# An mLSTM with an ELU feed-forward layer on one core: TensorE durations of a planner, its order, and small products of ones in TensorE's early gaps

## The chip, the core and the metric

The kernel runs on one core of a Trainium2 chip. The metric is the device time of one execution in microseconds (us), as the median of several runs; lower is better. Engines have the profile's names: PE is TensorE's matmuls and PEld its weight loads, DVE is VectorE, ACT is ScalarE, POOL is GpSimd, SP is SyncE, whose queue issues the transfers.

## What is computed

The reference is an mLSTM recurrence over 768 steps for 4 batches and 8 heads of 40, and then a feed-forward layer over the 3072 rows (320 wide, 2048 hidden):

```python
for t in range(S):
    m_new = np.maximum(f_gate[:, :, t] + m, i_gate[:, :, t])
    f_stab = np.exp(f_gate[:, :, t] + m - m_new)
    i_stab = np.exp(i_gate[:, :, t] - m_new)
    m = m_new
    C = f_stab[:, :, None, None] * C + i_stab[:, :, None, None] * np.einsum('bhd,bhe->bhde', vt, kt)
    n = f_stab[:, :, None] * n + i_stab[:, :, None] * kt
    h_tilde = np.einsum('bhde,bhe->bhd', C, qt)
    denom = np.maximum(np.abs(np.einsum('bhd,bhd->bh', n, qt)[:, :, None]), 1.0)
    y[:, :, t] = 1.0 / (1.0 + np.exp(-o_gate[:, :, t])) * h_tilde / denom
...
h = x @ w_in
g = np.where(h > 0.0, h, np.exp(np.minimum(h, 0.0)) - 1.0)
return g @ w_out
```

## The kernel before

**Tiles of the first part.** The recurrence is computed in chunks of 128 steps. There are 6 chunks and 4 batches, so 24 tiles, t0 to t23, with t0 to t3 the first chunk. For a tile the kernel loads queries and keys (`qk`), values with keys and the output gate (`vko`), and, from the second chunk on, decays that are spread over the partitions (`bb`). TensorE forms 16 products of queries and keys (`products`, L597). For the first two chunks it also makes the decay matrix in logarithms, twice per tile (`spread`: L628 adds a mask, L632 and L638 the gates' sums); ScalarE takes its exponential (L653), and VectorE multiplies the products by it (L662). Then TensorE forms the outputs and what is added to the state (`outputs`, L682, L690, L700). VectorE and ScalarE make the denominators (L733 to L742), the result (L746), and TensorE turns it (`turn`, L763) for the second part. The gates of a chunk are prepared for all four batches at once on VectorE in `gate_chunk` (L454 to L492); they end in `lcs`, which `spread` reads.

**The weights.** `w_in` and `w_out` come in 18 pieces, c0 to c17, 512 or 640 columns each. Every piece is taken apart into an upper and a lower part for two-part products; that is some work for VectorE (L336, L341, L346, L361), for ScalarE (L327, L332, L357) and for GpSimd (L351). Pieces c0, c1, c5 and c6 have their lower part made by TensorE (L369, L370). c0, c1 and c2 hold the first quarter of `w_in` (c2 also the last 64 rows of the second quarter), c5 and c6 the second quarter, c9, c10 and c11 the third; c3 and c4 hold the first quarter of `w_out`, c7 and c8 the second.

**The second part.** The tiles are joined to blocks of 2 or 3. For a block and 128 of the hidden columns, one step is: 8 matmuls of the first layer (L816), relu and exponential on ScalarE (L824, L827), a combination on VectorE (L829), the upper part of the result on ScalarE (L832), the lower on VectorE or GpSimd (L834), and 3 matmuls per tile of the second layer (L843) into `acc`. The first block does hidden columns 0 to 7 (in units of 128) first, as do the second and the third.

**What sets the order.** No order is written out by hand. Every operation is entered as an `op` with a duration for each engine that may do it, and with what it reads and writes. `Plan.run` simulates the engines, the transfers and the buffers with these durations: at each moment it starts the ready operation with the lowest `rank`, and among equals that with the longest tail behind it. At the end it calls the operations in the order of their simulated starts. So each engine's order of instructions is fixed before the kernel runs, and each engine takes its instructions in that order. A transfer of `nbytes` takes `nbytes / 235e3` us of a common queue, which begins at 0.7, and lands 1.6 us later; a result is seen by another engine after `HOP`, 0.1 us.

**Ranks.** A string, `FIRST`, gives the first tiles and pieces their ranks 0, 1, 2 and so on. What is not in it gets a rank by the step of the second part that needs it (`lead`), and each step ranks behind what it needs.

Of the kernel before, what the change touches and what calls it, by code (L numbers as in the profile page):

```python
# [13 lines left out]
BF16 = mybir.dt.bfloat16  # L14
# [6 lines left out]
P = 128  # L21
# [16 lines left out]
class Plan:  # L38
# [11 lines left out]
    RATE = 235e3  # L50
    DEEP = 3.0
    BEGIN = 0.7

    def __init__(self, room, in_turn=()):
        self.room, self.in_turn = room, in_turn
# [4 lines left out]
    def op(self, engines, fn, r=(), w=(), nbytes=0):  # L60
        port = "port" in engines
        engines = {e: x for e, x in engines.items() if e != "port"}
        o = Op(engines, fn, {k[:2] for k in (*r, *w)}, nbytes, port)
        o.rank = self.rank
        for k in r:
            if k in self.writer:
                o.before.add(self.writer[k])
            self.readers.setdefault(k, []).append(o)
        for k in w:
            if k in self.writer:  # L70
                o.before.add(self.writer[k])
            o.before.update(self.readers.pop(k, ()))
            self.writer[k] = o
        o.before.discard(o)
        for b in o.before:
            b.after.add(o)
        self.ops.append(o)
        return o

    def run(self):  # L80
# [18 lines left out]
        queue, port, t, order, events = 0.0, 0.0, 0.0, [], {0.0}  # L99
# [16 lines left out]
        while len(order) < len(self.ops):  # L116
            assert events, "nothing can go on"
            t = min(events)
            events.discard(t)
            again = True  # L120
            while again:
# [12 lines left out]
                for o in ready:  # L134
# [40 lines left out]
                    again = True  # L175
                    break
        self.end = max(engines.values())
        self.order = order
        for _, _, e, o in order:
            o.fn(e)  # L180
# [3 lines left out]
def tile_mlstm_then_elu_ffn(  # L184
# [9 lines left out]
    nc = tc.nc  # L194
    PSUM = bass.MemoryType.PSUM
    B, NC, R3, _, HH, L = qk.shape
    D = 40
    DM, DFF = w_in.shape[1], w_in.shape[0] * w_in.shape[2]
# [18 lines left out]
    TMAX = max(BLOCKS)  # L217
    WMAX = max(512, W2N * DM)

    FIRST = "t0c0c4t1c1c5t2t4c3c7c11c9"  # L220

    LEAD, SPACE, LEAD_C = 4, 3, 0

# [3 lines left out]
    room = dict(  # L227
        wide=3, narrow=2, gates=2, qk=3, bb=3, vko=3, w=3, wl=2, dec=2, den=2, xf=2,
        x=3, ps_a=3, h=2, acc=3, e=2, gh=4, gl=4, os=3,
    )  # L230
    plan = Plan(room, ("qk", "bb", "e", "gh", "gl", "os"))
    op = plan.op
# [31 lines left out]
    def T(name, i, *shape, dt=F32, part=""):  # L264

        if (name, i, part) not in tiles:
            tiles[name, i, part] = pools[name].tile(list(shape), dt, name=name + part)
        return tiles[name, i, part]
# [111 lines left out]
    minus = const.tile([P, P], F32R, name="minus")  # L380

    m0 = const.tile([BH, 1], F32, name="m0")

    first = const.tile([BH, L], F32, name="first")

# [17 lines left out]

    def setup():
        nc.scalar.preload_act_table_set("natural_log_exp_and_others")
        op({"DVE": 0.1}, lambda e: nc.vector.memset(m0, -1e30), (), (("m0", 0),))
        op({"POOL": 1.6}, lambda e: make_identity(nc, ident), (), (("ident", 0),))
        op({"POOL": 0.2}, lambda e: nc.gpsimd.memset(first, 0.0), (), (("first", 0),))
        op({"ACT": 0.3}, lambda e: nc.scalar.mul(minus, ident, -1.0), (("ident", 0),), (("minus", 0),))

        def select(e):
            for j in range(3):
                rows = slice(j * BH, (j + 1) * BH)
                eng[e].tensor_copy(sel[rows], ident[rows, rows])

        op({"port": 1, "POOL": 0.8, "DVE": 0.4}, select, (("ident", 0),), (("sel", 0),))
        op({"ACT": 0.3, "POOL": 0.3, "DVE": 0.2}, lambda e: copy(e, ident_b, ident), (("ident", 0),), (("ident_b", 0),))

        def masked(e):
            nc.gpsimd.memset(mask, 0.0)  # L420
            nc.gpsimd.affine_select(
                out=mask, in_=mask, pattern=[[1, L]], compare_op=ALU.is_ge, fill=MASKED, base=0,
                channel_multiplier=-1,
            )

        op({"POOL": 0.6}, masked, (), (("mask", 0),))
        op({"POOL": 0.7, "DVE": 0.6},
           lambda e: eng[e].tensor_copy(ident4, ident.unsqueeze(1).to_broadcast([P, HH, L])),
           (("ident", 0),), (("ident4", 0),))

        plan.rank = rank[f"t{B}"] - 0.001
        for j, t in enumerate(bbs):
            op({"DVE": 0.52, "POOL": 0.56},
               lambda e, t=t: eng[e].memset(t[32:64], 0.0), (), (("bbzero", j),))
        plan.rank = rank["t0"]
        for b in range(B):
            op({"DVE": 0.3, "POOL": 0.4},
               lambda e, b=b: eng[e].memset(C[b], 0.0), (), (("C", b),))
# [116 lines left out]
    def attention(n):  # L555
        c, b = divmod(n, B)
# [42 lines left out]
                        start=True, stop=True,  # L599
                    )  # L600

        op({"PE": 1.25}, products, KQ + (("w", n, "room"),), tuple(("ps_a", (n, two)) for two in range(2)))

        if c < LOGS:
            op({"POOL": 0.2, "DVE": 0.08}, lambda e: eng[e].memset(va()[:, :, D:E], 1.0), (), (KV,))
# [69 lines left out]
        def outputs(e):  # L675
# [28 lines left out]
                            )  # L704

        KY = ("ps_a", (n, "y"))
        op({"PE": (1.6 if c else 0.9) + (0.36 if c < NC - 1 else 0.0)}, outputs,
           (("w", n, 0), ("w", n, 1), KV) + (KB + (("C", b),) if c else ())
           + ((KK,) if c < NC - 1 else ()), (KY, ("given", n)))
        if c < NC - 1:  # L710
# [54 lines left out]
                    start=(t == 0), stop=(t == 2), is_transpose=True, skip_group_check=True,  # L765
                )

        op({"PE": 0.55}, turn, (("xf", n), ("ident", 0)), (KTP,))
        op(act(3 * L), lambda e: nc.scalar.copy(xs("h"), ps("tp", P, 3, L)),
           (KTP,), (KX + ("h", slot),))  # L770
        if n < PARTS_BY_PE[0]:
# [139 lines left out]
    at = 0.0  # L911
# [23 lines left out]
        conversion(i)  # L935
    for u, (kb, f0, f1) in enumerate(units):
        ffn(u, kb, f0, f1)
    plan.run()


# [40 lines left out]
```

## Time and profile before

| what | value |
|---|---|
| median of 3 runs | 475.62 us (474.58 to 477.79) |
| the profiled execution's own time | 479.09 us |
| its span, first to last instruction | 477.1 us |
| mean granted TensorE clock in it | 0.981 |
| PE busy | 456.9 us, 5692 matmuls |
| DVE busy | 347.8 us |
| ACT busy | 303.1 us |
| POOL busy | 89.5 us |

Times in the profile are those of one execution, counted from the first instruction. A row of the timeline gives the start, the time, the engine, the line and the operands of an instruction or of a row of like ones, and in brackets how long the engine was idle before and which engine's instruction ended the wait. A row of the stretches gives the length of a stretch, the busy time and number of instructions of each engine in it, the granted clock as a share of full speed, the share of the transfer engines' time and GB/s. Matmuls are pipelined, so the time of one is longer than its distance to the next.

### The profile page before, as it was taken

Reading aid. Unit: us, or ns where it says so; the run is one execution under the profiler, and the core shown is the slowest. Engines: PE = TensorE matmul, PEld = TensorE weight load, DVE = VectorE, ACT = ScalarE, POOL = GpSimd, SP = SyncE. Lnnn points to the kernel's source line nnn. Section 1 sums busy time; section 2 is a strip of 40 time slices with the busy share of each in tenths; the row PEclk is TensorE's granted clock in tenths of the full one; section 3 lists DMA queues with packets and bytes.
Section 4 is the critical chain, followed back from the end, with each engine's and each line's share of the span. In section 5 each row is a group of like instructions: output and inputs, shape, how many; then the busy total and the mean of one; then the engine's idle time right before and its main releaser. Section 6 shows DMA issues by size and latency. Waiting matters only on the chain.

```text
span 477.1 us, 13768 instructions
## 1 busy us (share of the span) xinstructions
PE 456.9 (96%) x5692; PEld 428.4 (90%) x5692; DVE 347.8 (73%) x729; ACT 303.1 (64%) x743; POOL 89.5 (19%) x103
## 2 busy tenths in 40 slices
PE   5977999999999989999999999999999999999996
PEld 3645889899999989999989999999999999999996
DVE  7897899997869899638995768648875475456543
ACT  5886788897876556646465546655546564645764
POOL 2421244433213131003040122102110010000000
PEclk9796999999999999999999999999999999999999
DMA  8777465534143394113642334404432030100000
GB/s 261 259 225 233 134 214 170 153 116 153 41 137 97 105 278 138 43 40 98 185 144 71 101 94 134 133 3 139 140 101 82 1 101 1 43 1 3 28 1 27
DMA packets 39389, 52.83 MB, mean 111 GB/s; under 512 B 2880, under 2 KB 31264, under 8 KB 39328
## 3 DMA queue, kind: packets, MB, share of 16 engines
q1 hardware_dynamic: 39328, 51.97, 35.2%
q8 instruction: 44, 0.72, 0.6%
q14 instruction: 17, 0.14, 0.1%
HBM read 46.56 MB, written 5.39 MB: 109 GB/s over the span
## 4 chain that ended last, share of the span: by engine, by line
PE 80%; DVE 10%; DMA 3%; issue 2%; ACT 2%; POOL 1%; SPq 1%; DVEq 0%; ACTq 0%
PE h L816 34%; PE acc L843 32%; PE ps_a L597 4%; PE ps_a L690 3%; PE ps_a L682 2%; DMA wide<-in_w_in 2%; PE ps_a L763 1%; DMA w<-f_d 1%; PE h L628 1%; PE ps_a L700 1%; PE h L632 1%; PE h L638 1%; DVE w L645 1%; DMA bb<-b_d 1%; DVE gl L834 1%
## 5 line engine op out<-in xcount | busy, mean ns | idle before, releaser
L816 PE MATMUL h<-xh,w 128*128 128x384 f32 (+1 forms) x720 | 179.1, 323 | 0.4 <-ACT e L827 0.2
L843 PE MATMUL acc<-w,gh 128*128 128x320 f32 x768 | 173.4, 312 | 0.1
L843 PEld LDWEIGHTS acc<-w,gh 128*128 128x128 f32 x768 | 127.8, 188 | 2.4 <-ACT gh L832 0.3
L816 PEld LDWEIGHTS h<-xh,w 128*128 128x128 f32 x720 | 125.6, 189 | 2.7 <-DVE e L829 1.0
L829 DVE SCALAR_TENSOR_TENSOR e<-e,h 128x384 f32<-128x384 f32 (+1 forms) x144 | 72.5, 505 | 69.8 <-ACT e L827 69.2
L843 PE MATMUL acc<-w,gl 128*128 128x320 f32 x384 | 118.7, 309 | 0.4 <-DVE gl L834 0.4
L824 ACT ACTIVATE e<-h 128x384 f32<-128x384 f32 (+1 forms) x144 | 65.4, 454 | 78.0 <-PE h L816 74.9
L816 PE MATMUL h<-xl,w 128*128 128x384 f32 (+1 forms) x432 | 112.0, 318 | 0.0
L832 ACT CAST gh<-e 128x384 fp32r<-128x384 f32 (+1 forms) x144 | 67.7, 473 | 35.1 <-DVE e L829 34.0
L834 DVE TENSOR_TENSOR gl<-e,gh 128x384 fp32r<-128x384 f32 (+1 forms) x122 | 66.3, 547 | 32.1 <-ACT gh L832 30.2
L816 PEld LDWEIGHTS h<-xl,w 128*128 128x128 f32 x432 | 76.9, 189 | 0.0
L827 ACT ACTIVATE e<-e 128x384 f32<-128x384 f32 (+1 forms) x144 | 70.5, 490 | 4.0
L843 PEld LDWEIGHTS acc<-w,gl 128*128 128x128 f32 x384 | 72.0, 188 | 0.9 <-DVE gl L834 0.8
L834 POOL TENSOR_TENSOR gl<-e,gh 128x384 fp32r<-128x384 f32 (+1 forms) x22 | 24.4, 1115 | 109.0 <-ACT gh L832 95.6
L645 DVE TENSOR_TENSOR_SCAN w<-w,ident 128x512 f32<-128x512 f32 x32 | 39.1, 1225 | 4.6 <-DMA w<-f_d 4.6
L615 ACT ACTIVATE vko<-vko 128x320 f32<-128x320 f32 x72 | 33.5, 467 | 7.7 <-DMA vko<-in_vko 7.2
L597 PE MATMUL ps_a<-qk 40*128 40x128 f32 x384 | 31.0, 304 | 6.4 <-DMA qk<-in_qk 5.1
L351 POOL TENSOR_TENSOR narrow<-narrow,wide 128x512 int32<-128x512 int32 (+1 forms) x18 | 26.5, 1474 | 55.5 <-DVE narrow L346 25.9
L597 PEld LDWEIGHTS ps_a<-qk 40*128 40x128 f32 x384 | 25.9, 204 | 11.6 <-DMA qk<-in_qk 5.1
L662 DVE TENSOR_TENSOR w<-ps_a,w 128x512 f32<-128x512 f32 x48 | 31.6, 682 | 3.1 <-PE ps_a L597 2.7
L690 PE MATMUL ps_a<-vko,w 128*32 128x41 f32 x1536 | 20.3, 207 | 0.0
L690 PEld LDWEIGHTS ps_a<-vko,w 128*32 128x32 f32 x1536 | 18.6, 114 | 1.2 <-issue 1.1
(104 smaller groups left out, 413.9 us busy)
## 6 DMA issues: line engine op xcount, KB each, us to landing
vko<-in_vko SPq DMA_DIRECT2D x24, 484.0 KB
qk<-in_qk SPq DMA_DIRECT2D x24, 448.0 KB
w<-f_d SPq DMA_DIRECT2D x32, 256.0 KB
wide<-in_w_out SPq DMA_DIRECT2D x8, 640.0 KB
wide<-in_w_in SPq DMA_DIRECT2D x8, 512.0 KB
out<-os SPq DMA_DIRECT2D x24, 160.0 KB
bb<-b_d SPq DMA_DIRECT2D x40, 80.0 KB
sum<-os SPq DMA_DIRECT2D x8, 160.0 KB
```

The source lines that it names most:

```text
L597: nc.tensor.matmul(ps(two, P, HH, L)[:, j, :], kt[rows, j, :], qt[rows, j, :], start=True, stop=True,)
L615: lambda e, fn=fn, kw=kw: nc.scalar.activation(v3()[2], v3()[2], fn, **kw), (), (KS,))
L645: nc.vector.tensor_tensor_scan(a, a, ident4.rearrange("p h t -> p (h t)"), 0.0, op0=ALU.mult, op1=ALU.add)
L662: lambda e, half=half: nc.vector.tensor_mul(w(half), ps(half, P, HH, L), w(half)),
L690: nc.tensor.matmul(y[r, h, :], w()[:, i, r], va()[:, h, :], start=not opened, stop=(i == H - 1), skip_group_check=True,)
L816: nc.tensor.matmul(h(), a[g][:, fs], m, start=(i == 0), stop=(i == len(prods) - 1))
L824: op(act(N), lambda e, h=h, ff=ff: nc.scalar.activation(ff("e"), h(), AF.Relu, scale=-1.0), (KHP,), (KE,))
L827: lambda e, ff=ff: nc.scalar.activation(ff("e"), ff("e"), AF.Exp, scale=-1.0), (), (KE,))
L829: lambda e, h=h, ff=ff: nc.vector.scalar_tensor_tensor(out=ff("e"), in0=ff("e"), scalar=-1.0, in1=h(), op0=ALU.add, op1=ALU.max),
L832: op(act(N), lambda e, ff=ff: nc.scalar.copy(ff("gh", F32R), ff("e")), (KE,), (KG,))
L834: lambda e, ff=ff: eng[e].tensor_sub(ff("gl", F32R), ff("e"), ff("gh", F32R).bitcast(F32)),
L843: nc.tensor.matmul(acc(a), x[:, sl], bw[g][:, j, :], start=(f == f0 and i == 0), stop=(f == f1 - 1 and i == 2),)
```

## The change

Three things change. The planner's durations for `products`, `outputs` and `turn` on TensorE become shorter. `FIRST` becomes `t0 c0 c4 t1 c1 t2 t3 t4 c3 c7 c10 c11`: c5 and c9 leave it, t3 and c10 come in, and t3 stands ahead of t4. And a filler is added: a tile `ones` of 128 x 192 in bf16 is set to one, first on VectorE; when the plan is made, every gap on TensorE between the moment at which `ones` is there and the start of the first second-layer operation is given as many products of ones (128 rows, 128 weight columns, 192 columns) as fit in it less 0.1 us. They are counted at 0.165 us in the first gap and 0.09 us in the later ones. They write to columns of `acc` that nothing reads. They are not part of the simulation: it is over when they are put in, at the place in TensorE's order at which the gap begins.

```diff
+    FILL, FILL_COLD = 0.09, 0.165
+    filler = fill_from = fill_until = None
...
         self.end = max(engines.values())
+        if self.filler:
+            until = min(t for t, _, _, o in order if self.fill_until in o.touched)
+            begin = at = min(t + o.engines[e] for t, _, e, o in order if self.fill_from in o.touched) + self.HOP
+            more = []
+            for t, number, e, o in order:
+                if e == "PE" and t <= until:
+                    count = int((t - at - 0.1) / (self.FILL_COLD if at == begin else self.FILL))
+                    if count > 0:
+                        x = Op({"PE": t - at}, lambda e, count=count: self.filler(count), set(), 0, False)
+                        more.append((at, number, e, x))
+                    at = t + o.engines[e]
+            order = sorted(order + more, key=lambda x: x[0])
         self.order = order
...
-    FIRST = "t0c0c4t1c1c5t2t4c3c7c11c9"
+    FIRST = "t0c0c4t1c1t2t3t4c3c7c10c11"
...
+    ones = const.tile([P, 512 - DM], BF16, name="ones")
...
+        plan.rank = -1.0
+        op({"DVE": 0.1}, lambda e: nc.vector.memset(ones, 1.0), (), (("ones", 0),))
+        plan.rank = 0.0
...
-        op({"PE": 1.25}, products, KQ + (("w", n, "room"),), tuple(("ps_a", (n, two)) for two in range(2)))
+        op({"PE": 1.16}, products, KQ + (("w", n, "room"),), tuple(("ps_a", (n, two)) for two in range(2)))
...
-        op({"PE": (1.6 if c else 0.9) + (0.36 if c < NC - 1 else 0.0)}, outputs,
+        op({"PE": (1.38 if c else 0.8) + (0.32 if c < NC - 1 else 0.0)}, outputs,
...
-        op({"PE": 0.55}, turn, (("xf", n), ("ident", 0)), (KTP,))
+        op({"PE": 0.49}, turn, (("xf", n), ("ident", 0)), (KTP,))
...
+    def busy_work(count):
+        spare = T("acc", (0, 0), P, 512)[:, DM:]
+        for _ in range(count):
+            nc.tensor.matmul(spare, ones[:, 0:P], ones, start=True, stop=True, skip_group_check=True)
+
+    plan.filler, plan.fill_from, plan.fill_until = busy_work, ("ones", 0), ("turn", 2)
     plan.run()
```

## The prediction, made before the changed kernel ran

> **What bounds the kernel now.** I read the page first, then the busy time of each engine by stretches, then TensorE's timeline of the first 60 us, then VectorE's and what its idle time waited for. The page:
>
> ```profile
> span 477.1 us, 13768 instructions
> PE 456.9 (96%) x5692; PEld 428.4 (90%) x5692; DVE 347.8 (73%) x729; ACT 303.1 (64%) x743; POOL 89.5 (19%) x103
> PE   5977999999999989999999999999999999999996
> PEclk9796999999999999999999999999999999999999
> ```
>
> TensorE is busy 96% of the span and nearly all of its slack is in the first four slices of twelve us (and in the last, the drain). There the granted clock falls too. The stretches between its changes, and the rest of the run (columns: us in the stretch, PE, PEld, DVE, ACT, POOL busy, clock, DMA):
>
> ```profile
> 0.00:5.09 5.09, 0.00 (x0) 0.00 (x0) 3.75 (x15) 2.26 (x6) 2.26 (x11) 1.00 0.56 164
> 5.09:12.08 6.99, 6.70 (x36) 4.21 (x37) 4.85 (x17) 4.16 (x8) 0.40 (x1) 1.00 1.03 333
> 12.08:18.90 6.82, 5.67 (x139) 3.91 (x137) 5.33 (x13) 5.77 (x15) 2.40 (x3) 1.00 0.93 308
> 18.90:25.72 6.82, 6.82 (x122) 5.03 (x122) 5.64 (x15) 4.83 (x13) 2.93 (x3) 0.50 0.52 164
> 25.72:39.38 13.66, 8.04 (x136) 4.89 (x135) 12.99 (x34) 12.20 (x30) 3.39 (x3) 1.00 0.76 234
> 39.38:49.62 10.24, 8.89 (x135) 7.27 (x135) 7.27 (x18) 5.59 (x13) 2.53 (x3) 0.50 0.82 238
> 49.62:100.00 50.38, 49.62 (x825) 44.86 (x824) 46.48 (x97) 42.72 (x102) 18.88 (x19) 1.00 0.54 168
> 100.00:477.10 377.10, 371.19 (x4307) 358.19 (x4305) 261.47 (x527) 225.58 (x562) 56.73 (x61) 1.00 0.28 86
> ```
>
> From 49.62 on TensorE waits 0.76 us in 50 and 5.91 us in 377: whatever is gained ahead of 49.62 should stay gained, and little is to be had behind it. Two stretches show a clock of 0.50. A third is slow although its column says 1.00, which the durations show (TensorE's timeline: start, us, then the instruction):
>
> ```profile
> 5.09 2.08 PE L597 MATMUL ps_a<-qk 40*128 40x128 f32 x16 [5.09 <-DMA qk<-in_qk]
> ...
> 8.00 0.61 PE L632 MATMUL h<-sel,lcs 96*128 96x512 bf16 x1 [0.29 <-DVE lcs L490]
> 8.40 0.63 PE L638 MATMUL h<-lcs,sel 96*128 96x128 bf16 x4
> 8.83 0.63 PE L628 MATMUL h<-mask,ident_b 128*128 128x512 bf16 x1
> ...
> 12.61 0.38 PE L632 MATMUL h<-sel,lcs 96*128 96x512 bf16 x1
> 12.83 0.39 PE L638 MATMUL h<-lcs,sel 96*128 96x128 bf16 x4
> ...
> 14.94 1.16 PE L597 MATMUL ps_a<-qk 40*128 40x128 f32 x16
> ```
>
> The same 16 products take 2.08 us at 5.09 and 1.16 us at 14.94, so TensorE starts at half clock and keeps it until about 12. Cold busy time is 6.70 + 6.82 + 8.89 = 22.4 us; at full clock it would be 11.2. That is the most that a warm clock can give, and only if nothing else ended the waits. But in the front VectorE is nearly full: 12.99 of 13.66 us between 25.72 and 39.38. So what counts is VectorE's idle time that a cold TensorE caused (timeline of VectorE, idle before and its releaser in brackets):
>
> ```profile
> 9.70 0.17 DVE L236 COPY wl<-w 128x4 f32<-128x4 f32 x1 [1.62 <-ACT w L653]
> 14.31 0.67 DVE L236 COPY C<-ps_a 40x164 f32<-40x164 f32 x2 [1.01 <-PE ps_a L700]
> 22.72 1.29 DVE L662 TENSOR_TENSOR w<-ps_a,w 128x512 f32<-128x512 f32 x2 [0.54 <-PE ps_a L597]
> 24.48 0.67 DVE L236 COPY C<-ps_a 40x164 f32<-40x164 f32 x2 [0.40 <-PE ps_a L700]
> 42.84 0.17 DVE L236 COPY wl<-w 128x4 f32<-128x4 f32 x1 [0.41 <-ACT w L653]
> 44.12 0.17 DVE L236 COPY wl<-w 128x4 f32<-128x4 f32 x1 [0.77 <-ACT w L653]
> 45.49 1.29 DVE L662 TENSOR_TENSOR w<-ps_a,w 128x512 f32<-128x512 f32 x2 [1.21 <-PE ps_a L597]
> 50.17 0.42 DVE L829 SCALAR_TENSOR_TENSOR e<-e,h 128x256 f32<-128x256 f32 x1 [0.91 <-ACT e L827]
> ```
>
> Those released by ScalarE go back to TensorE as well: ScalarE's exponentials wait for the spread products, its relu for the first layer.
>
> **When the clock falls and rises.** Its visible changes lie on a grid of 3.41 us (18.90, 25.73, 39.38, 49.62), so I asked for the stretches of that grid:
>
> ```profile
> 15.49:18.90 3.41, 2.26 (x22) 1.34 (x18) 3.28 (x7) 3.36 (x8) 0.00 (x0) 1.00 0.97 329
> 18.90:22.32 3.42, 3.42 (x23) 2.49 (x23) 3.21 (x7) 3.39 (x10) 1.29 (x1) 0.50 0.52 160
> 29.14:32.55 3.41, 2.01 (x8) 0.96 (x10) 3.28 (x9) 3.22 (x9) 1.29 (x1) 1.00 1.02 280
> 35.97:39.38 3.41, 1.23 (x4) 0.47 (x3) 3.14 (x11) 2.56 (x7) 0.00 (x0) 1.00 0.58 202
> 42.79:46.21 3.42, 3.42 (x69) 2.97 (x71) 1.39 (x6) 2.49 (x5) 0.72 (x1) 0.50 0.83 238
> ```
>
> The clock fell behind stretches with 2.26 and 1.23 us of matmul, and not behind one with 2.01; it did not rise behind 18.90:22.32 or 42.79:46.21 although TensorE was full there, with two us of 40-row products in each. Busy time alone does not decide; what the array is given seems to count. The filler has 128 rows, so I expect it to count fully, which no row here shows.
>
> The longest gaps of TensorE ahead of the two falls:
>
> ```profile
> 17.05 0.67 PE L763 MATMUL ps_a<-ident,xf 128*128 128x128 f32 x3 [0.94 <-DVE xf L746]
> ...
> 40.73 0.59 PE L628 MATMUL h<-mask,ident_b 128*128 128x512 bf16 x1 [3.53 <-DVE e L829]
> ```
>
> The Trainium skill (TensorE: Matmul & The Clock Gate, section "Why this matters for your kernels") speaks against filling short gaps: only gaps above about 3 us are to bring the clock back to half. The trace differs, since the fall at 18.90 follows a gap of 0.94 us. By the rule that fall would have another cause than idling, the fill would not mend it, and the sum below would be the second stretch's 0.94 us smaller.
>
> **The change part by part.**
>
> *Fill at the head.* By its own constants the plan has the first products at about 4.49 us (0.7 to the queue's begin, 2.09 of gate and query bytes, 1.6 of landing, 0.1), the fill from 0.2, so (4.49 - 0.2 - 0.1) / 0.165 = 25 fillers. Their price: the four products of 128 columns at 8.40 take 0.43 us to the next start, 0.107 each cold, and one of 512 columns from 8.00 to 8.40 takes 0.40 to 0.43; by the line through both, 192 columns take about 0.16 us cold, and half of that warm. 25 of them are 4.0 us from about 1.1, so they end at 5.1 at the latest, where the products' data lands (5.09): free. If the clock has risen by 8.00, where the chain turns from VectorE's decay sums to TensorE, the first exponential comes 0.5 us earlier, and the first outputs 0.7 us earlier still (of the 1.01 at 14.31; ScalarE, 5.77 of 6.82 us busy behind 12.08, takes the rest of the 2 us that TensorE saves).
>
> *Second stretch.* Warm products and outputs give VectorE back 0.54 + 0.40 = 0.94 us.
>
> *Third stretch.* Of 0.41 I take 0.30, and 0.77 + 1.21 + 0.91 whole: 3.19 us. Halving TensorE's 8.89 us would allow 4.4; VectorE's own work takes the difference.
>
> Together 0.5 + 0.7 + 0.94 + 3.19 = 5.3 us, between nothing (clock as before) and 11.2 (TensorE alone decides).
>
> *What the fillers cost.* TensorE takes its instructions in order. A filler stands where the plan, not the chip, has a gap. In 5.09 to 49.62 TensorE is idle about 8.4 us now (the stretches' lengths less PE's time, rows above), and some 14 once its work there is 11.2 us shorter and the front 5.3; at 0.09 a filler, less what the rounding leaves, that is some 130 fillers.
>
> ```profile
> 29.99 0.96 DVE L737 TENSOR_SCALAR den<-den 128x8 f32<-128x8 f32 x1
> ```
>
> VectorE runs behind its plan there (this maximum and the reciprocal behind it are planned at 0.30 together), so most gaps will be as long as planned or longer, and the filler ends before the data. Where TensorE itself is late, a filler adds its length. Bounds: 0 and 5.2 us (half of 130 at 0.08 us, the excess when cold). I take 0.6, near the lower end, because VectorE is the fuller engine in the front. The memset of ones, first on VectorE, costs the 0.1 of its plan, and the chain starts on VectorE, so it counts whole. The head's rise may come too late for the first exponentials: 0 to 1.2, taken as 0.5.
>
> The Trainium skill (the same page, section "Part 1: The HAM clock gate") has one busy window of 3.4 us raise the clock. By that the head's fill has the clock up by 8.5 us at the latest; by the rows of 18.90:22.32, with 40-row products behind the fill, it may be a window later, and then the sum is 0.7 us less.
>
> *Order anew.* c5 (a quarter of w_in) leaves the ranks of the front, t3 comes ahead of t4, c10 stands in for c9 (same size). c5's steps now, with its transfer:
>
> ```profile
> 31.46 0.39 DVE L336 TENSOR_SCALAR narrow<-narrow 128x512 f32<-128x512 f32 x1
> 31.88 0.43 DVE L341 TENSOR_SCALAR narrow<-narrow 128x512 int32<-128x512 int32 x1
> 32.34 0.69 DVE L346 SCALAR_TENSOR_TENSOR narrow<-wide,narrow 128x512 int32<-128x512 int32 x1
> 20.45 0.33 SPq L322 DMA_DIRECT2D wide<-in_w_in  x1
> 50.27 0.46 PE L843 MATMUL acc<-w,gh 128*128 128x320 f32 x2
> ```
>
> 1.5 us of VectorE leave the stretch in which VectorE is full, and its transfer falls behind those of t2, t3, t4 and c3 on SP's queue. But it is needed for the fifth step of the first block, and between 49.62 and 100 VectorE has 46.48 of 50.38 us; t3's steps come forward in its place. Bounds +1.5 and -1.5; I take 0, as work is only exchanged.
>
> *Durations.* The plan's TensorE shrinks by 24 x 0.09 + 20 x 0.26 + 4 x 0.14 + 24 x 0.06, some 9 us; 1.16 for the products is what the row at 14.94 shows. No instruction changes, only the order of a greedy list. Behind 49.62 there are 6.7 us of idle TensorE in all, the drain behind the last matmul among them; so at best some 2 us, at worst a wait of the size of the front's, 1.2 us. I take 0.
>
> **The sum.** 5.3 - 0.1 - 0.6 - 0.5 = 4.1 us. The profiled execution took 479.09 us, of which 477.1 are its span: 475.0 after. The three runs shown have a median of 475.62, 3.5 us below the profiled one. If that offset belongs to profiling, the median becomes 471.5, which is my forecast. If it is the clock (the grid need not lie alike in every execution, and the runs spread over 3.2 us), the median has less cold time to lose; that is the second rival.
>
> **Rivals.**
> 1. *More than the clock.* VectorE's waits all close (the eight rows hold 6.87 us, of which 1.0 of the first stays: a spread and its exponential at full clock, 5.9 us), and c5's 1.5 us stay out of the front: 7.4, so 468.2. For it: VectorE is the full engine there, and TensorE has 8.4 us idle to take up. Against: VectorE has little room until 100.
> 2. *The median has little cold time.* The third stretch costs most and may not occur in a run whose grid splits the idle 3.5 us otherwise. Then 4.1 - 3.2 = 0.9 stay: 474.7. For it: the spread of the runs. Against: the idle time at the head and around 40 is there whatever the grid.
> 3. *Slower: fillers in the way.* If the clock stays at half where the plan counts 0.09, each of 130 fillers takes 0.08 more, 10.4 us, and half of that meets work that is ready: 5.2 us later with nothing gained, 480.8. It decides once more than 50 fillers' excess (4.1 us) falls on work that is ready. For it: full busy stretches that did not raise the clock. Against: those were 40-row products, and VectorE's waits are longer than the plan's.
>
> **How the numbers follow.** Forecast 0.47, rival 1 0.20, rival 2 0.22, rival 3 0.11. A measurement of this kernel tells about 1% from no change, 4.76 us: below 470.9 or above 480.4. The forecast's own spread of 2 us puts some four tenths of it below: 0.47 x 0.4 + 0.20 = 0.39, rounded to 0.40 faster; rival 3 lies on the border, 0.07 slower; 0.53 within. The range goes from rival 1 less a us, 467, to 477, which holds rival 2 with the runs' spread and leaves out rival 3 and the far end of rival 1.
>
> **What would show it.** Right: a group of some 130 to 180 matmuls with 192 columns ahead of the first L843; the products at 5.09 still 2 us or less but the spread from 8.0 in steps of 0.22; clock 1.00 to 50; VectorE's idle rows above gone or halved; the first second-layer matmul near 45 to 46 instead of 50.27; idle time behind it unchanged. Wrong: a stretch at 0.50 in spite of the fill; a filler directly ahead of a TensorE instruction whose data was long there; a first second-layer matmul that is early while the end is not, which would mean that VectorE became the bound between 50 and 100.

## The result and the profile after

The changed kernel takes 484.02 us (median of 4 runs, 482.68 to 485.93) against 476.65 of the kernel before on the same chip: ratio 1.0146, 95% interval 1.0105 to 1.0187. It is 1.5% slower, and lies outside the forecast's range. The profiled execution took 485.93 us, the most of the four; the one of before, 479.09 us, also lies above that kernel's median. A few executions, 1.5% or more above the fastest of their kernel (the profiled one of e4 below by far the most, 1110.94 us), are left out of every ratio. The page of the changed kernel:

```profile
span 483.9 us, 14087 instructions
PE 468.2 (97%) x5842; PEld 441.2 (91%) x5842; DVE 353.1 (73%) x741; ACT 301.7 (62%) x738; POOL 85.1 (18%) x97
PEclk9889999999999989999999999999999999999999
q8 instruction: 46, 0.75, 0.6%
```

The first four slices are warmer than before (9, 8, 8, 9 against 9, 7, 9, 6); a new dent in the clock stands at slice 15. The stretches of the prediction, cut at 100, 150 and 200 us (columns as there):

```profile
0.00:5.09 5.09, 3.97 (x25) 3.60 (x25) 3.77 (x15) 2.26 (x6) 2.27 (x11) 1.00 0.58 170
5.09:12.08 6.99, 6.96 (x70) 5.55 (x69) 4.84 (x18) 4.20 (x9) 0.18 (x1) 1.00 1.04 317
12.08:18.90 6.82, 5.09 (x138) 4.01 (x136) 5.92 (x13) 4.89 (x12) 2.75 (x3) 1.00 0.99 304
18.90:25.72 6.82, 6.82 (x46) 5.17 (x46) 4.17 (x9) 5.37 (x13) 3.04 (x3) 0.58 1.03 290
25.72:39.38 13.66, 13.66 (x381) 11.25 (x379) 11.50 (x35) 9.05 (x25) 2.28 (x3) 0.96 0.49 161
39.38:49.62 10.24, 8.48 (x87) 7.43 (x87) 9.29 (x22) 7.85 (x19) 2.41 (x3) 1.00 0.65 200
49.62:100.00 50.38, 48.17 (x802) 42.52 (x801) 47.25 (x101) 41.82 (x98) 15.08 (x14) 1.00 0.55 171
100.00:150.00 50.00, 49.32 (x332) 48.04 (x332) 44.72 (x82) 40.92 (x93) 14.12 (x12) 1.00 0.38 122
150.00:200.00 50.00, 46.69 (x651) 44.31 (x650) 39.53 (x77) 25.27 (x72) 10.34 (x11) 0.93 0.45 125
200.00:483.90 283.90, 279.01 (x3330) 269.26 (x3328) 182.09 (x379) 160.07 (x397) 32.67 (x37) 1.00 0.24 72
```

Idle TensorE between 49.62 and 100 went from 0.76 to 2.21 us, and 150:200 has 3.31 us idle and a clock of 0.93. The kernel before, in the same stretches:

```profile
100.00:150.00 50.00, 49.95 (x342) 49.32 (x341) 41.56 (x83) 40.18 (x93) 14.52 (x12) 1.00 0.35 112
150.00:200.00 50.00, 48.73 (x672) 46.52 (x671) 43.59 (x85) 29.13 (x80) 9.26 (x11) 1.00 0.45 134
```

The head did what the change says. TensorE's timeline after (the line numbers move: products L615, outputs L708 and L718, second layer L861, fillers L960):

```profile
1.12 4.18 PE L960 MATMUL acc<-ones 128*128 128x192 bf16 x25 [1.12 <-DVE ones L422]
5.24 1.69 PE L615 MATMUL ps_a<-qk 40*128 40x128 f32 x16
6.85 1.74 PE L960 MATMUL acc<-ones 128*128 128x192 bf16 x19
8.43 0.38 PE L646 MATMUL h<-mask,ident_b 128*128 128x512 bf16 x1
8.65 0.38 PE L650 MATMUL h<-sel,lcs 96*128 96x512 bf16 x1
```

25 fillers end nearly in time for the first products (5.24 against 5.09), and the spread products run in steps of 0.22 instead of 0.40 us. The fill stops being good at 16 us, where TensorE stands still within a row of like products, and something else breaks at 174:

```profile
15.64 0.93 PE L615 MATMUL ps_a<-qk 40*128 40x128 f32 x10
18.30 0.49 PE L615 MATMUL ps_a<-qk 40*128 40x128 f32 x4 [1.73 <-issue]
...
45.30 0.38 PE L646 MATMUL h<-mask,ident_b 128*128 128x512 bf16 x1 [1.76 <-DVE e L847]
...
50.40 0.57 PE L861 MATMUL acc<-w,gh 128*128 128x320 f32 x2
...
172.68 0.78 PE L700 MATMUL ps_a<-C,bb 104*32 104x82 f32 x32
173.28 0.79 PE L708 MATMUL ps_a<-vko,w 128*32 128x41 f32 x63
173.88 0.48 PE L718 MATMUL ps_a<-vko 128*8 128x41 f32 x30
177.67 0.23 PE L718 MATMUL ps_a<-vko 128*8 128x41 f32 x1 [3.31 <-issue]
177.83 0.64 PE L861 MATMUL acc<-w,gh 128*128 128x320 f32 x1
```

In the middle of one `outputs` call, whose operands have all been there since its first matmul, TensorE stands still for 3.31 us, and the profile names no releaser ("issue"). Then the clock is at half (a 1.80 us stretch, the stand, and the 6.30 us behind it):

```profile
172.40:174.20 1.80, 1.80 (x130) 1.55 (x129) 1.52 (x3) 0.42 (x1) 1.01 (x1) 1.00 1.02 345
174.20:177.60 3.40, 0.16 (x17) 0.03 (x3) 0.91 (x3) 1.26 (x3) 0.99 (x1) 0.92 0.93 285
177.60:183.90 6.30, 6.23 (x22) 6.08 (x22) 4.49 (x8) 2.23 (x8) 3.07 (x3) 0.50 0.68 191
```

The half clock is only a part of the loss. The mean clock was 0.986 in this execution and 0.992 to 0.996 in the three others, and they still took 482.68 to 484.95 us.

**What "issue" was.** The kernel before has one such wait too:

```profile
PE ps_a L597 <- issue: 1.3, 1, 1.3
q8 instruction: 44, 0.72, 0.6%
```

I counted TensorE's instructions in the trace: a matmul is two, a weight load and the product, and the semaphore instructions between them count as well. At every such wait of a matmul of over 1 us, in all traces here but that of e4, the count stands at 191 or 192 above a multiple of 256: before at 4288 (16 x 256 + 192), after at 448 (16.30 us) and 4543 (174.16 us). The instruction queue moves packets of 16384 bytes, 44 before and 46 after, one for every 256 instructions. So TensorE's program arrives in blocks of 256 instructions, and at the end of one it can go on only when the next has landed. Such an end is called a border here. In after's trace the border ahead of the stand is passed at 172.68; the block's transfer starts at 175.27, in the midst of a DMA share of 0.93 to 1.02, and lands at 176.32; TensorE goes on at 177.67. Most blocks take 5 to 20 us, and the transfer is hidden. But an `outputs` call is 256 instructions in 1.7 us: where one block is nearly one `outputs` call and the DMA engines are full, the block ends before the next is there. 150 fillers are 300 instructions, that is one block and 44 instructions: they move every later border to another place in the work.

The Trainium skill (Runtime: NRT & Kernel Launch, section "Instruction fetch mechanics") says the same of the blocks: 16 KiB, 256 instructions, the next fetched while the present one runs, the crossing mostly hidden. The trace agrees with the size and the order. "Mostly hidden" holds for all block ends but two in the trace of the changed kernel, and not where a block lasts 1.5 us under full transfers: 3.5 us there.

### The profile page after: what moved, and what is told of

It is laid out like the page before. It is cut to its first block, busy times and chain, and to the rows that moved or that the text cites. A ratio compares the mean times of both kernels' runs of the same rounds, so it can differ in the third digit from the quotient of the medians.

```text
span 483.9 us, 14087 instructions
## 1 busy us (share of the span) xinstructions
PE 468.2 (97%) x5842; PEld 441.2 (91%) x5842; DVE 353.1 (73%) x741; ACT 301.7 (62%) x738; POOL 85.1 (18%) x97
## 4 chain that ended last, share of the span: by engine, by line
PE 82%; DVE 10%; DMA 2%; ACT 2%; issue 2%; SPq 0%; DVEq 0%; ACTq 0%
PE h L834 32%; PE acc L861 32%; PE ps_a L615 5%; PE acc L960 3%; PE ps_a L708 3%; PE ps_a L700 2%; DMA w<-f_d 2%; DVE gl L852 1%; DVE e L847 1%; PE ps_a L781 1%; PE ps_a L718 1%; PE h L383 1%; DVE w L663 1%; DMA bb<-b_d 1%; DVE narrow L360 1%
## 5 line engine op out<-in xcount | busy, mean ns | idle before, releaser
L861 PE MATMUL acc<-w,gh 128*128 128x320 f32 x768 | 175.0, 314 | 0.2
L861 PEld LDWEIGHTS acc<-w,gh 128*128 128x128 f32 x768 | 129.1, 190 | 6.2 <-issue 3.6
L861 PE MATMUL acc<-w,gl 128*128 128x320 f32 x384 | 119.3, 311 | 0.5 <-DVE gl L852 0.4
L861 PEld LDWEIGHTS acc<-w,gl 128*128 128x128 f32 x384 | 72.6, 189 | 1.3 <-DVE gl L852 1.3
L663 DVE TENSOR_TENSOR_SCAN w<-w,ident 128x512 f32<-128x512 f32 x32 | 40.9, 1280 | 5.5 <-DMA w<-f_d 5.4
L615 PE MATMUL ps_a<-qk 40*128 40x128 f32 x384 | 29.8, 295 | 1.7 <-issue 1.7
L615 PEld LDWEIGHTS ps_a<-qk 40*128 40x128 f32 x384 | 24.9, 197 | 6.7 <-issue 5.3
L708 PE MATMUL ps_a<-vko,w 128*32 128x41 f32 x1536 | 19.5, 202 | 0.0
L960 PE MATMUL acc<-ones 128*128 128x192 bf16 x150 | 17.4, 278 | 1.1 <-DVE ones L422 1.1
```

Of the source, the lines that this page charges most:

```text
L615: nc.tensor.matmul(ps(two, P, HH, L)[:, j, :], kt[rows, j, :], qt[rows, j, :], start=True, stop=True,)
L663: nc.vector.tensor_tensor_scan(a, a, ident4.rearrange("p h t -> p (h t)"), 0.0, op0=ALU.mult, op1=ALU.add)
L708: nc.tensor.matmul(y[r, h, :], w()[:, i, r], va()[:, h, :], start=not opened, stop=(i == H - 1), skip_group_check=True,)
L861: nc.tensor.matmul(acc(a), x[:, sl], bw[g][:, j, :], start=(f == f0 and i == 0), stop=(f == f1 - 1 and i == 2),)
L960: nc.tensor.matmul(spare, ones[:, 0:P], ones, start=True, stop=True, skip_group_check=True)
```

## The experiments

To tell where time goes I used one measure for all traces, the work done: each of the kernel's own matmuls counts with its usual step (the median spacing of its kind in the kernel before, behind 52 us); fillers count nothing. At a given time, the work done less that of the kernel before is a kernel's lead. The table has how much the lead grows (+) or shrinks (-) in three parts of the span, in us, from one profiled execution each. A stand is a time in which TensorE starts nothing; the last column has the longest at a block's end, from one start to the next less the usual step, which is up to 0.2 us more than the idle time that the profile gives in brackets.

| kernel | ratio to before, 95% interval | 0 to 50 | 50 to 150 | 150 to 400 | longest stand at a block's end, us |
|---|---|---|---|---|---|
| after | 1.0146 [1.0105, 1.0187] | +2.1 | -4.0 | -4.8 | 3.50 at 174, 1.90 at 16 |
| e1: fillers alone, 153 | 1.0113 [1.0061, 1.0166] | +1.3 | +0.6 | -5.2 | 3.18 at 170, 2.63 at 29 |
| e2: FIRST alone | 0.9966 [0.9932, 1.0001] | +1.2 | -0.2 | +2.7 | 2.04 at 33 |
| e3: durations alone | 1.0108 [1.0065, 1.0151] | +2.7 | -7.0 | +0.8 | 2.51 at 62 |
| e4: change less fillers | 1.0048 [1.0015, 1.0080] | | | | |
| e5: e1 less its last 41 | 1.0035 [0.9991, 1.0079] | +2.7 | -0.6 | -1.0 | 1.37 at 16 |
| e6: 25 at the head alone | 1.0052 [1.0005, 1.0099] | -0.1 | +0.6 | -5.5 | 4.02 at 172 |
| e7: change less its last 16 | 1.0137 [1.0071, 1.0202] | -1.2 | -5.6 | +0.1 | 1.83 at 16, 1.39 at 82 |
| e8: FIRST and 120 fillers | 0.9967 [0.9931, 1.0003] | +2.0 | -1.0 | +1.8 | 2.45 at 34 |
| e9: change and 18 more | 1.0182 [1.0129, 1.0236] | +0.4 | -3.7 | -3.9 | 3.58 at 175 |
| e10: e1 less 33, borders moved | 0.9956 [0.9925, 0.9987] | +5.5 | 0.0 | +0.8 | 0.36 at 177 |
| e11: FIRST and 116, borders moved | 0.9948 [0.9915, 0.9980] | +2.0 | -0.7 | +1.4 | 2.53 at 23 |
| e12: durations and 116, borders moved | 1.0111 [1.0056, 1.0167] | +5.4 | -7.5 | -1.0 | 2.89 at 59 |
| e13: change less 22, borders moved | 1.0077 [1.0041, 1.0113] | +1.8 | -4.4 | +0.5 | 2.67 at 24 |
| e14: e12 less 9 | 1.0091 [1.0048, 1.0135] | +2.2 | -5.5 | -0.1 | 1.71 at 62 |
| e15: e4 again, one execution (482.42 us) | | +0.1 | -4.4 | +0.9 | 1.45 at 28 |

**The three parts apart (e1 to e4).** Each kernel is the one before with one part, or the changed one without the fillers:

```diff
 e1  FIRST = "t0c0c4t1c1c5t2t4c3c7c11c9", durations 1.25 / 1.6, 0.9, 0.36 / 0.55, with fillers
 e2  FIRST = "t0c0c4t1c1t2t3t4c3c7c10c11", the rest as before
 e3  durations 1.16 / 1.38, 0.8, 0.32 / 0.49, the rest as before
 e4  the change without
-    plan.filler, plan.fill_from, plan.fill_until = busy_work, ("ones", 0), ("turn", 2)
```

> The kernel before with the fillers alone: old durations, old order string; the order of all other work on every engine is that of before, to the instruction. Theory A (TensorE's instruction fetch: 300 more instructions in its stream move the places where the next block of instructions is fetched late, a stall of 3.5 us follows and the clock falls behind it): about 480 to 484 us, with a wait of TensorE of 2 us or more that no other engine ended. Theory B (the new order of the list is what costs; the fill by itself does what it was meant to): 470 to 474 us, clock 1.00 in the front, the first second-layer matmul two us or more earlier than 50.27. Theory C (the fill is worth nothing because VectorE sets the front): 475 to 478 us.

> The kernel before with the new order string alone, no fillers, old durations. Theory A: 474 to 477 us, as before. Theory B: 479 us or more, with TensorE waiting for VectorE between 50 and 150. Theory C says nothing of it.

> The kernel before with the three new TensorE durations alone, no fillers, old order string. Theory A: 474 to 477 us. Theory B: slower than before if the shorter durations are what spoils the order, 478 to 482 us; about 476 if the order string is.

> The changed kernel without the fillers (its tile of ones is still set): every other instruction of every engine in the same order as in the changed kernel. Theory A: 475 to 478 us, so that the fillers explain the whole loss of about 7 us. Theory B: 484 us or more, since the cold stretches of the front come on top of the worse order.

Measured 483.24, 475.95, 483.43 and 479.88 us, beside 476.82 of the kernel before. FIRST costs nothing. Fillers alone and durations alone cost 1.1% each, and fillers on top of the rest 1%. The parts do not simply add: with the new FIRST the durations cost 0.5% (e4), which is between the two ranges expected there. The fillers change no other instruction's place on any engine, so e1 is the kernel before with a memset and 153 products put in between, and it is still ahead at 150 us. Its waits:

```profile
PE ps_a L718 <- issue: 5.4, 2, 3.0
PE ps_a L615 <- issue: 1.5, 1, 1.5
```

Of the 5.2 us that it loses behind 150, 3.4 go between 165 and 180, at the stand. Another 2.4 go between 240 and 250, where it waits 0.77 and 1.30 us for VectorE; the kernel before waits 0.42 us for VectorE there.

**Is it the number of instructions? (e5 to e8.)** Fewer fillers move the borders. e5 and e7 leave out the last ones, e6 keeps those of the first gap only (50 instructions, where TensorE has nothing else to do), e8 puts 120 into e2:

```diff
+    LIMIT, spent = 112, []        (e5 on e1; 25 in e6 on e1, 134 in e7 on the change, 120 in e8 on e2)
     def busy_work(count):
+        count = min(count, LIMIT - len(spent))
         for _ in range(count):
+            spent.append(0)
```

> The kernel before with 112 fillers instead of the 153 of the fill-only kernel: the last 41 are left out, everything else is the same to the instruction. TensorE's instructions are fetched in blocks of 256 of 64 bytes; 112 fillers are 224 instructions, so behind the front the block borders lie 32 instructions later than in the kernel before, where its trace shows no row of small products that empties a block within 4.5 us of full transfers. Theory A (fetch at block borders): 472 to 475 us, no wait of 1 us or more inside a row of like products behind 50, clock 1.00 there. Rival (the fillers themselves delay work, in proportion to their number): 481 to 482 us, three quarters of the 6.4 us stay. Rival (the front's gain is real but VectorE gives it back near 240): 478 to 480.

> The kernel before with the 25 fillers of the head alone, where TensorE has nothing to do. 25 fillers are 50 instructions, and 153 are 306, which is 256 and 50: so behind the front the block borders lie just where they lie in the fill-only kernel. Theory A: a wait of 2 to 3.5 us inside the outputs near 170, the clock at half behind it, 479 to 483 us. Rival (fillers in the way): as before or better, 474 to 477 us, since none stands between the work.

> The changed kernel with 134 fillers instead of 150 (the last 16 left out), 32 instructions less in front, so that the border that fell into the outputs at 174 falls into the first and second layer. Theory A: 477 to 480 us, at or below the 479.9 of the changed kernel without fillers, no long wait near 174. Rival (fillers in the way): 483 to 484 us.

> The kernel before with the new order string and 120 fillers (10 less than the plan gives), old durations; 240 instructions, so that the borders behind the front lie 16 instructions later than in the order-only kernel, away from its rows of small products. Theory A: 472 to 475 us, faster than both kernels. Rival (fillers in the way): 480 us or more. Rival (VectorE sets the front, the fill gives nothing): 475 to 477 us.

Measured 478.45, 480.54, 485.48 and 476.80 us, beside 478.63. e6 is the plainest. Its 25 fillers can delay next to nothing, and its work is level with the kernel before until 150; its timeline:

```profile
170.84 0.79 PE L708 MATMUL ps_a<-vko,w 128*32 128x41 f32 x63
171.45 0.46 PE L718 MATMUL ps_a<-vko 128*8 128x41 f32 x27
175.74 0.25 PE L718 MATMUL ps_a<-vko 128*32 128x41 f32 x4 [3.83 <-issue]
```

The stand is back at instruction 4287, in `outputs`; its ten runs spread over 477.83 to 484.65 us, and the profiled one is the slowest, so the trace shows more than the usual loss. e5 and e8, which have the same head and over 110 fillers, have no such stand at 170 and lose nothing between 165 and 200. So it is not the fillers' time that costs, but where the border falls. e7 missed: the stand at 174 went (0.96 at 182 is left) and gave 3.5 us back, but without the last fillers TensorE fell to half clock between 45 and 52 and lost them again; it stayed at 1.0137. e5 and e8 missed theory A's 472 to 475 us too, and lie in the range of a rival: the front's gain was not there. In e5, without its last fillers, the clock is at half from 40.50 to 47.33; e8 has two waits for "issue" of 2.3 us, at 16 and 34.

**Moving the borders on purpose (e9 to e12).** The number of fillers per gap is written out, so that blocks end in slow work:

```diff
+    COUNTS = iter([25, 4, 4, 4, 12, 3, 11, 0, 9, 16, 10, 22])      (e10; e1 has 25, 18, 4, 4, 12, 3, 11, 19, 9, 16, 10, 22)
     def busy_work(count):
-        for _ in range(count):
+        for _ in range(next(COUNTS)):
```

e9 has 37 instead of 19 in the change's last gap; e11 is e2 with 25, 4, 4, 4, 12, 3, 11, 14, 6, 1, 31, 1; e12 is e3 with 25, 4, 4, 4, 13, 5, 10, 16, 8, 7, 0, 3, 17.

> The changed kernel with 18 fillers more than it has, all in its last gap (37 in place of 19, ahead of the spread products that waited 1.76 us at 45.30). 36 instructions more: the block border that fell into the outputs at 174 falls elsewhere. Theory A (fetch at block borders): no wait of 2 us or more inside the outputs near 174 and no cold stretch behind it, 479 to 482 us although there are more fillers. Rival (fillers in the way): 484 us or more.

> The fill-only kernel with 120 of its 153 fillers: 14 of the 18 behind the first products are left out, so that the second block border passes behind t1's products near 16 (in all filled kernels so far they stood still there for 1.4 to 2.4 us), and the 19 near 27. 240 instructions, so behind the front no border lies in a row of small products. Theory A: no wait at the products near 16, at 100 us TensorE at least 2.5 us ahead of the profile of before, none above 1.5 us at a border later; the end 474 to 477 us, since some 2 us are given back where TensorE waits for VectorE near 245. Rival (the clock is worth nothing): as before, 477 to 479 us.

> The order-only kernel with fillers, 116 of the 130 that its plan gives (14 of the 18 behind the first products left out). The border that stopped t1's products for 2.4 us at 16 and the one that stopped the outputs for 2.4 us at 34 both pass behind them. Theory A: neither wait; 472 to 475 us, below both kernels and below the order-only kernel. Rival (VectorE sets the front): 475 to 477 us, as the order-only kernel.

> The durations-only kernel with fillers, 116 of the 169 that its plan gives, chosen so that the borders that stopped its outputs for 2.5 us at 61 and 1.3 us at 188 lie elsewhere, and the one near 16 behind t1's products. Theory A (the loss of the shorter durations is a border in the outputs and the cold time behind it): 476 to 479 us. Rival (the order that the shorter durations give is worse by itself): 481 to 484 us, with TensorE's waits for VectorE at 43 and 74 still there.

Measured 486.13, 475.43, 474.99 and 482.62 us, beside 478.51. e10 has the same order as e1, 33 fillers fewer, and 1.6% less time. The same place in its trace:

```profile
165.48 0.79 PE L708 MATMUL ps_a<-vko,w 128*32 128x41 f32 x63
166.09 0.49 PE L718 MATMUL ps_a<-vko 128*8 128x41 f32 x31
166.51 0.44 PE L834 MATMUL h<-xh,w 128*128 128x384 f32 x1
...
169.48 1.04 PE L615 MATMUL ps_a<-qk 40*128 40x128 f32 x13
170.68 0.49 PE L615 MATMUL ps_a<-qk 40*128 40x128 f32 x3 [0.15 <-issue]
```

The transfer is as late as in the changed kernel (border at 165.42, start at 168.34, landed at 169.32, TensorE free at 170.68, 1.36 us later), but the block now holds 3 us of first-layer products, and 0.15 us of wait is left. In the front nothing stands still at a block's end either (the clock is at half once, from 29.17 to 32.58), and the first second-layer matmul comes where the prediction had it:

```profile
45.22 0.45 PE L861 MATMUL acc<-w,gh 128*128 128x320 f32 x2
```

e11 is within theory A's range by 0.01 us, but a new stand of 2.53 us at 23 came for the two that left, and its ratio (0.9948) is not told apart from that of FIRST alone (0.9966). e9 missed: 36 instructions are too few to take a border out of 256 of them. TensorE stood at the same number, 4543, 18 matmuls earlier in the same `outputs` call, for 3.58 us. e12 missed too, and it is what brought the second cause out: at 50 us it is 5.4 us ahead, at 100 it is behind.

**The order that the durations make (e13 to e15).** e13 is the change with 25, 4, 4, 4, 6, 5, 10, 16, 28, 7, 19 fillers; e14 is e12 with 4 instead of 13 in the fifth gap; e15 is e4's kernel.

> The change with 22 of its 150 fillers left out ahead of 16 us (15 in the second gap, 7 in the fifth), all others kept. TensorE's 256-instruction borders then fall 44 instructions later in the work: the ones that stood still for 1.90 us at 16 and 3.50 us at 174 fall into slower work. Theory A (the change loses by where TensorE's instruction blocks end): both stands and the half-clock stretches behind them go; of the 1.9 + 3.5 + 3.4 us some 5 to 7 arrive at the end: 477 to 480 us. Rival B (the order that comes from the new durations and ranks is itself slower, by waits for VectorE): 481 to 484 us even without a stand above 1 us.

> The kernel before with the three durations and 107 fillers: the run with 116 less nine in the fifth gap (14.5 us), so that its border at 58.9 us, where TensorE stood for 2.89 us, falls 18 instructions later, where the block takes over 5 us. Theory A: the stand at 59 goes, the clock stays up behind it and the wait for VectorE near 72 shrinks: 476 to 479 us. Rival B (the durations' order is slow by itself): the wait of 2.0 us near 72 stays or grows by what the stand leaves, 481 to 483 us.

> The change without its fillers (the ones are still set), a look at its trace alone: time about 480 as measured before. Theory A: its loss of about 2 us against the kernel before lies in a stand of TensorE at a border of 256 instructions under full transfers, of 1.5 us or more. Rival B: no such stand, and the loss lies in waits of TensorE for VectorE between 50 and 100 us.

Measured 481.10, 482.47 and 482.42 us, beside 477.80. e13 has no stand above 0.6 us behind 27 us and gained half of the change's loss (1.0146 to 1.0077), as the block theory says; the other half stayed, as its rival says, and the time lies in the rival's range. e14's stand shrank from 2.89 to 1.71 us, and the wait behind it did not:

```profile
PE acc L861 <- DVE w L375: 1.8, 1, 1.8
PE ps_a L718 <- issue: 1.5, 1, 1.5
```

e15, with no filler at all, is level at 50 us and 4.2 us behind at 150; the theory's stand of 1.5 us under full transfers is there (1.45 at 28), but it lies ahead of 50 and is not what it loses by. (This one execution is slower than the nine executions in e4's ratio, 478.89 to 481.70 us, so its trace may show more than the usual loss. e13's profiled execution, 480.95 us, lies at its median.) TensorE between 50 and 150 us, in the kernel before, in e10, in e13 and in e15:

```profile
50.00:150.00 100.00, 99.20 (x1162) 93.81 (x1161) 88.03 (x179) 82.56 (x193) 33.40 (x31) 1.00 0.44 140
```

```profile
50.00:150.00 100.00, 99.53 (x1152) 94.52 (x1151) 86.92 (x179) 81.39 (x191) 33.84 (x32) 1.00 0.46 139
```

```profile
50.00:150.00 100.00, 96.80 (x1127) 89.67 (x1124) 91.19 (x182) 82.65 (x191) 28.83 (x26) 1.00 0.48 148
```

```profile
50.00:150.00 100.00, 96.39 (x1130) 89.22 (x1129) 89.58 (x179) 82.18 (x191) 28.06 (x25) 1.00 0.46 142
```

3.2 and 3.6 us idle against 0.8 and 0.5, at full clock. The column of the table says the same: all eight kernels with the new durations lose 3.7 to 7.5 us between 50 and 150, and none of the seven with the old ones loses more than 1.1, with and without fillers, with the old FIRST and the new. In e3, e12 and e14 a stand of 1.7 to 2.9 us is part of it; after, e13 and e15, with none above 1.1 there, lose 4.0 to 4.4. More work for VectorE in all is not the reason: the changed plan gives it more (353.1 us busy against 347.8, and GpSimd six operations fewer), but in e3, e12 and e14 VectorE has less than before (344.6 to 344.9), and they lose as much.

## Why the prediction was wrong

The loss of the profiled execution, 485.93 - 479.09 = 6.84 us, is +2.1 - 4.0 - 4.8 = -6.7 in the table.

1. *The gain, 5.3 us.* Its mechanism held: the head's rise came by 8.43 us, the first products were 0.15 us late, and e10, with the fillers as its only change and no stand, is 5.5 us ahead at 50 and has its first second-layer matmul at 45.22. That "whatever is gained ahead of 49.62 should stay gained" is also so in e10 (6.3 us at 400). In the changed kernel 2.1 us of the gain are there, and that matmul comes at 50.40. Against it stand the 1.73 us in the products at 16.30, the half clock that follows (0.58 in 18.90:25.72, the "stretch at 0.50 in spite of the fill" of the prediction's last list) and the wait of 1.76 us at 45.30. VectorE, whose waits were to close, got new ones in that stretch:

```profile
24.79 1.29 DVE L680 TENSOR_TENSOR w<-ps_a,w 128x512 f32<-128x512 f32 x2 [2.15 <-PE ps_a L615]
27.72 0.67 DVE L250 COPY C<-ps_a 40x164 f32<-40x164 f32 x2 [1.64 <-PE ps_a L718]
```

The head's rise is not certain either. With the same 25 products, e13 and e14 had their spread products in steps of 0.43 us until 10.2, the later rise that the prediction allowed for; e13:

```profile
8.44 0.63 PE L650 MATMUL h<-sel,lcs 96*128 96x512 bf16 x1
8.87 0.63 PE L656 MATMUL h<-lcs,sel 96*128 96x128 bf16 x4
```

2. *What the fillers cost, 0.6 us.* This step failed. It priced their time in TensorE's order and nothing else. Their number, 300 instructions, was never carried into the sum: it moves the ends of TensorE's blocks. Of the 4.8 us lost behind 150, 4.4 go between 165 and 185, at the stand and in the half clock behind it, beside the 2 us of the stand at 16. Rival 3 had a loss by the fillers of the right sign, by another mechanism; e6 and e10 tell the two apart, as 25 fillers where TensorE has nothing to do lose, and 120 whose borders fall well gain.

3. *Durations, 0 us, bounds -2 to +1.2.* This step failed too. The bound took "a wait of the size of the front's, 1.2 us"; the measured -4.0 between 50 and 150 is made of waits for VectorE and ScalarE and of steps slightly longer throughout (2.8 us more than before in steps that are over 0.2 late, 1.3 in smaller ones, counted as for the work done). The waits that the changed kernel's timeline names there:

```profile
61.98 0.39 PE L834 MATMUL h<-xh,w 128*128 128x256 f32 x1 [0.37 <-ACT w L387]
72.02 0.44 PE L834 MATMUL h<-xh,w 128*128 128x384 f32 x1 [1.16 <-DVE e L847]
99.79 0.42 PE L861 MATMUL acc<-w,gl 128*128 128x320 f32 x1 [0.45 <-DVE gl L852]
```

VectorE's work in 49.62:100 rises from 46.48 to 47.25 of 50.38 us. The prediction itself named 49.62 to 100 as a stretch in which VectorE has little room, and still priced an order with less TensorE time in it at nothing. Why the list made from truer TensorE durations is worse is not settled: VectorE's durations stayed as they were, and the row at 29.99 in the prediction shows them too short there; that this is the cause was not tried.

4. *Order anew, 0 us (+-1.5).* Right: e2 is within 0.4% of the kernel before, and the 2.7 us that it gains behind 150 are that kernel's own stand of 1.44 us at 175 and what followed it.

5. *The offset of 3.5 us and rival 2.* e10's profiled execution (472.22) is the fastest of its twelve, whose median is 475.43: of the 6.9 us that it gains on the profiled execution of before, 0.4%, some 2 us, is left between the medians. Rival 2's price of 0.9 us is nearer to this than the forecast's 4.1, but its reason, a median with little cold time, is not what the recorded clocks show. On that chip the kernel before had a median clock of 0.985, against 0.981 in the profiled execution; the share lost times the span is 7.1 and 9.1 us, and 1.4 us in e10's median. So some 2 us of the cold time was the profiled execution's own, and 5.7 us went between the medians. Why only 2 us of these arrive in the time stays open.

A first second-layer matmul "that is early while the end is not" was also in that list, with VectorE between 50 and 100 as the reason. The changed kernel does not show it; e12, 5.4 us ahead at 50 and 1.1% slower at the end, does.

## What to carry to other kernels

Instructions have a place as well as a duration: before adding or removing any on TensorE, count them, and look where the ends of its blocks of 256 fall; a block of short matmuls under full transfers is where a late one shows, and some 20 fillers more or fewer can move it (22 fewer did in e13, 18 more did not in e9). Waits for "issue" at a fixed remainder of the instruction count are its mark. And this greedy order was not improved by making one engine's durations truer; time the new order by itself (e3 here) before adding to it.

The version to keep is e11: FIRST anew and 116 fillers with the old durations, 0.9948 of the kernel before, or e10, 0.9956; both intervals lie below 1. FIRST alone (e2, 0.9966) has no fillers to place, and the runs do not tell it apart from these two.

## What the runs showed of the hardware

- One transfer of 16384 bytes per 256 instructions of TensorE, taking 0.9 to 2.1 us. The traces, without that of e4, have 25 block ends at which TensorE started nothing for over 1 us. There the transfer began 0.7 to 6.5 us behind the border, and TensorE went on 1.2 to 1.7 us after it had landed. At 24 of them the transfer engines' share was 0.77 or more in the 2 us behind the border; the exception is 1.17 us in e7 at 286. Where the share was under 0.3, nearly all transfers began between 2.5 us ahead of the border and 1.4 us behind it.
- Blocks of 1.5 us cost 0.1 us or less with light transfers (e9 at 220 and 345, e10 at 276). Blocks of 1.2 to 2.1 us cost 2.0 to 4.0 us with full ones (after at 174, e1 at 170, e2 at 33, e6 at 172, e8 at 34), and 1.7 us at a share of 0.77 (e9 at 69).
- Behind the stands of 3.2 to 4.0 us near 170 (after, e1, e6, e9) the clock fell to half, for one or two steps of the 3.41 us grid. In after it was 0.50 from 177.04 to 183.87 us with TensorE full (the row 177.60:183.90 above), which is some 3.4 us of work lost on top of the stand.
- 25 products of ones from 1.12 us on had the clock up at 8.43 at the latest in after, and not before 10.2 in e13 and e14. In after it was down again from 20.03, behind the stretch 12.08:18.90, whose only idle time is the 1.73 us at 16.
